# Strassen's seven products for the second layer of an attention and gelu-MLP kernel

## The chip, the core and the metric

The kernel runs on one core of one Trainium2 chip. The metric is the device time of one execution in microseconds. TensorE (PE) multiplies, VectorE (DVE), ScalarE (ACT) and GpSimd (POOL) work on tiles, and DMA queues move data, those of SyncE (SP) and of GpSimd here. Each engine takes its instructions in the order in which they were written, and waits for the others by semaphores. Operands lie in SBUF, results of TensorE in PSUM.

## The reference

Attention over 8 batches, 12 heads, 448 tokens and a head width of 64, with q and k normalised by their root mean square, and behind it a two-layer perceptron on the 3584 tokens. All inputs are float32 and the output is float32.

```python
q_n, k_n = rmsnorm(q, g_q), rmsnorm(k, g_k)
scores = 1/sqrt(64) * q_n @ k_n.T
attn = softmax(scores)                   # over keys
x = (attn @ v) as (8*448, 768)           # heads side by side
h = x @ w_in                             # 768 -> 2048
g = gelu_tanh(h)
out = g @ w_out                          # 2048 -> 768
```

## The kernel before

Tokens of a batch are taken as 7 blocks of R = 64 (token number modulo 7 gives the block), heads as three chunks of four (c = 0 to 2). Matmuls are in bfloat16. The weights `win` and `wout` stay in SBUF; `g` holds the gelus of two batches. Nearly all matmuls of the steady part use a quarter of the array, 64 rows by 64 columns, so that four of them run side by side.

The work on a batch b goes in two alternating stretches. In the **first layer** of batch b (`mm1_turn`, L537) TensorE makes eight pairs of 128 rows of h, ScalarE turns each into `g` (L543), GpSimd normalises q and k of the next batch (`normed`, L278), DMAs transpose them into `qT` and `kT`, and VectorE multiplies `kT` by the gains (`gain`, L325) and sums squares (`total`, L173). In the **attention phase** of batch b + 1 (`attention`) TensorE weaves two things together: scores and products of batch b + 1, and the second layer of batch b.

The order on TensorE in that phase is written by hand, as words of a string (`STEADY` for batches 2 to 7, `SECOND` for batch 1). `u` is one of 21 units (`unit`, L335): the scores of 64 keys of a chunk, four matmuls of 448 columns into a PSUM pair; ScalarE takes their exps (`exp`, L343). `s` and `x` (`products`, L387) are the sums of the exps and the product with V of a chunk, the latter 28 matmuls. `5r` is five steps of the second layer, four matmuls each of 384 columns (`quartered`, L495); the last 32 steps of a phase have 192 columns.

A second string gives VectorE's order for the three chunks: A, B, F and G add exps of 7 key blocks into `es` (L355, L358, L360, L362) so that `s` needs four matmuls; T transposes the sums (`turned`, L397), R takes reciprocals (L402), S spreads them (L409), M multiplies the product with V into `xT` (L422). E is an eviction of a finished second-layer tile (`evict`, L513), on VectorE or at a place in ScalarE's order given by the dict behind the strings. `go_on` writes an instruction of VectorE or ScalarE as soon as what it needs has been written (`needs`). So the words fix each engine's order, and semaphores the times.

PSUM is four pairs of banks, `rounds`. `u`, `s` and `x` take the pair at the front and put it at the back; the second layer takes one out for as long as it sums into it. Whoever takes a pair waits for its last reader: an exp, T, M or an eviction.

`follows` makes TensorE drain before the two halves of the array's rows swap their banks. `final` does the last second layer, on the whole array (L463). `gpsimd_waits` (L800) is a one-element copy that holds GpSimd back until the last add of exps in a phase.

## Time and profile before

| | before |
|---|---|
| median of 3 runs | 390.82 us (389.91 to 391.95) |
| span of the profiled execution | 389.1 us |
| TensorE busy | 381.8 us |
| ScalarE busy | 278.2 us |
| VectorE busy | 242.0 us |
| GpSimd busy | 126.1 us |
| mean granted TensorE clock | 1.000 |

The profile is of one execution, whose own device time is not listed apart from its span, from the first to the last instruction; the listed runs lie 0.8 to 2.9 us above that span. A row of a timeline gives the start, the length, the engine, the line, the operation, what it writes and reads with the shape of one, and how many instructions are merged. Matmul rows overlap, since a matmul's recorded end lies after the next one's start; what a group takes of TensorE is read from one start to the next.

### The profile page before, as it was taken

Reading aid. Unit: us, or ns where it says so; the run is one execution under the profiler, and the core shown is the slowest. Engines: PE = TensorE matmul, PEld = TensorE weight load, DVE = VectorE, ACT = ScalarE, POOL = GpSimd, SP = SyncE. Lnnn points to the kernel's source line nnn. Section 1 sums busy time; section 2 is a strip of 40 time slices with the busy share of each in tenths; the row PEclk is TensorE's granted clock in tenths of the full one; section 3 lists DMA queues with packets and bytes.
Section 4 is the critical chain, followed back from the end, with each engine's and each line's share of the span. In section 5 each row is a group of like instructions: output and inputs, shape, how many; then the busy total and the mean of one; then the engine's idle time right before and its main releaser. Section 6 shows DMA issues by size and latency. Waiting matters only on the chain.

```text
span 389.1 us, 17513 instructions
## 1 busy us (share of the span) xinstructions
PE 381.8 (98%) x8044; PEld 296.3 (76%) x8044; DVE 242.0 (62%) x367; ACT 278.2 (71%) x351; POOL 126.1 (32%) x109
## 2 busy tenths in 40 slices
...
GB/s 258 326 232 210 210 222 239 260 175 192 209 44 106 256 197 60 76 154 257 133 64 65 189 253 103 47 115 241 110 68 61 121 48 42 44 65 4 2 81 83
...
## 3 DMA queue, kind: packets, MB, share of 16 engines
...
q0 software_dynamic: 10128, 11.80, 18.3%
...
## 4 chain that ended last, share of the span: by engine, by line
PE 92%; ACT 4%; DMA 1%; POOL 1%; SPq 0%; DVE 0%; issue 0%; DVEq 0%
PE t L537 33%; PE t L495 32%; PE t L387 9%; PE t L335 7%; PE t L463 5%; PE t L556 4%; ACT ex L343 4%; DMA rawq<-in_q_dram 1%; POOL g L164 1%; PE h L436 1%; PE o L387 0%; PE tp L296 0%; SPq L750 0%; DVE ss L173 0%; PE os L387 0%
## 5 line engine op out<-in xcount | busy, mean ns | idle before, releaser
L343 ACT ACTIVATE ex<-t,shift 128x896 bf16<-128x896 f32 x168 | 156.2, 1012 | 2.6 <-PE t L335 2.1
L495 PE MATMUL t<-wout,g 64*64 64x384 bf16 (+1 forms) x3456 | 152.0, 305 | 0.0
L495 PEld LDWEIGHTS <-g 64*64 64x64 bf16 x3456 | 115.3, 107 | 17.7 <-issue 0.2
L537 PE MATMUL t<-xT,win 64*64 64x448 bf16 x2688 | 128.7, 349 | 0.0
L537 PEld LDWEIGHTS <-win 64*64 64x64 bf16 x2688 | 97.8, 107 | 29.4
L543 ACT ACTIVATE g<-t 128x896 bf16<-128x896 f32 x56 | 50.5, 915 | 56.8 <-PE t L537 56.7
L173 DVE TENSOR_REDUCE ss<-sq 128x14 f32<-128x896 f32 (+3 forms) x45 | 44.3, 999 | 48.7 <-ACT sq L162 46.4
L335 PE MATMUL t<-qT,kT 64*64 64x448 bf16 x672 | 59.7, 352 | 1.9 <-ACT ex L343 0.6
L800 POOL COPY mark<-es 1x1 bf16<-1x1 bf16 x7 | 1.2, 177 | 134.9 <-DVE es L362 126.6
L278 POOL TENSOR_TENSOR nrmq<-rawq,rinv 128x896 bf16<-128x896 f32 (+1 forms) x21 | 34.8, 1659 | 18.8 <-ACT rinv L205 8.4
L355 DVE TENSOR_TENSOR es<-ex 128x1792 bf16<-128x1792 bf16 x21 | 22.2, 1059 | 29.5 <-ACT ex L343 29.5
L278 POOL TENSOR_TENSOR nrmk<-rawk,rinv 128x896 bf16<-128x896 f32 (+1 forms) x21 | 34.6, 1647 | 0.0
L387 PE MATMUL t<-ex,vb 64*64 64x448 bf16 x588 | 32.4, 350 | 0.2 <-issue 0.2
L335 PEld LDWEIGHTS <-kT 64*64 64x64 bf16 x672 | 26.1, 106 | 8.1 <-DVE kT L305 2.0
L397 DVE STREAM_TRANSPOSE st<-t 128x448 f32<-128x448 f32 x42 | 24.8, 628 | 9.2 <-PE t L387 9.2
L387 PEld LDWEIGHTS <-vb 64*64 64x64 bf16 x672 | 23.2, 107 | 8.3 <-issue 1.8
L409 DVE STREAM_TRANSPOSE rb<-rc 128x896 f32<-128x896 f32 (+1 forms) x25 | 26.7, 1068 | 0.3
L706 DVE COPY osb<-t 128x384 f32<-128x384 f32 (+1 forms) x4 | 2.0, 508 | 35.2 <-PE t L463 35.2
L422 DVE TENSOR_TENSOR xT<-t,rb 128x896 bf16<-128x896 f32 x21 | 22.8, 1087 | 0.9
L513 ACT COPY osb<-t 128x768 f32<-128x768 f32 (+1 forms) x18 | 12.6, 700 | 14.0 <-PE t L495 14.0
L358 DVE TENSOR_TENSOR es<-es,ex 128x1792 bf16<-128x1792 bf16 x21 | 22.3, 1062 | 0.0
L164 POOL TENSOR_TENSOR sq<-rawq 128x896 f32<-128x896 f32 (+1 forms) x9 | 13.6, 1510 | 24.1 <-DVE ss L173 17.4
...
## 6 DMA issues: line engine op xcount, KB each, us to landing
...
win<-in_moe_w_in_dram POOLq DMA_DIRECT2D x8, 384.0 KB, 11.1
...
```

The costliest lines, as they stand in the source:

```text
L173: nc.vector.reduce_sum(sss[b][:, seat(b, c), "qk".index(n), hs, ts], squares(b, c, n, hs, ts), axis=AX.X)
L278: eng.tensor_mul(nrms[n, b, c][:, ts].rearrange("p t a d -> p a t d"), raws[n, b, c][:, :, ts], root[:, :, ts].to_broadcast([P, 2, m, D]),)
L335: nc.tensor.matmul(sc[r * R:(r + 1) * R, a, :S], kT[rs, c, t, r], qT[b][rs, c, :, r], start=True, stop=True,)
L343: nc.scalar.activation(exs[b, c][:, t], scs.pop((b, c, t))[:, :, :S], AF.Exp, scale=scale, bias=shift)
L358: nc.vector.tensor_add(es, es, ex[:, 4:6])
L387: nc.tensor.matmul(o[r][a * D:(a + 1) * D], vb[b % 2][rs, 2 * c + a, i] if what else ones[rs], es[i][rs, a], start=(i == 0), stop=(i == n ...
L397: nc.vector.transpose(st[:, r].rearrange("p a b -> p (a b)"), o[r])
L409: nc.vector.transpose(oas["rb"][:, rs].rearrange("p r s -> p (r s)"), rc.to_broadcast([128, (rs.stop - rs.start) * m, 32]),)
L422: nc.vector.tensor_mul(xT[b][:, 2 * c:2 * c + 2], oas["o", c, 1][:, :, :S], oas["rb"])
L495: mm = nc.tensor.matmul(o[a * R:(a + 1) * R, bank, :hi - lo], g[rs, f, at:at + R], wout[rs, f, lo:hi], start=(n == 0), stop=(n == len(step ...
L537: mm = nc.tensor.matmul(h[a * R:(a + 1) * R, j, :S], win[rs, c, at:at + R], xT[b][rs, c], start=begin and c == cs[0], stop=end and c == cs ...
L543: nc.scalar.activation(g[:, 2 * i:2 * i + 2, (b % 2) * S:(b % 2 + 1) * S], h[:, :, :S], AF.Gelu_apprx_tanh,)
```

## The change

The second layer of a batch, 448 tokens by 2048 by 768, is computed for batches 1 to 7 by Strassen's method in the form with seven products: six token blocks are halved into three and three (A1, A2), the 2048 into even and odd groups of 128, the 768 columns into halves. Seven products of half size in each direction stand for eight. The seventh token block (64 tokens) is done apart, in as many matmuls as before, with the sum of its two halves ("L") and B12 - B22. Batch 0 is done directly (`direct`), now with its last block within the same phase.

Sums of the gelus (`summands`): "S", three instructions on VectorE, "4" and "L" on GpSimd, each for halves of j: the first in the first layer, the others at the phase's head. Sums of the weights (`weight_sums`): three on GpSimd of 3072 elements a partition during the attention phase of batch 1, one on VectorE, in place, in the first layer of batch 1.

The products are combined when they are evicted: `scalar_part` (a), `vector_part` (e) and `gpsimd_part` (g), with numbers k = 0 to 3 for the products of token blocks 0 and 1 over 384 columns, 4 to 7 for the third block, 8 for the seventh block (`evict_rest`). Of the products, k = 0 holds numbers 2 and 1, k = 1 numbers 5 and 6, k = 2 numbers 3 and 7, k = 3 number 4 in two halves; 4 to 7 likewise. The steps of k = 0 to 2 are 16 each, of 384 columns; the others are eight matmuls of 192 columns a step: 8 for each of k = 3 to 6, and 20 for k = 7 and 8 together, which hold two PSUM pairs.

To make room, `g`, `xT`, `es` and V (`vb`) have one buffer each; the scratch of the first squares lies in the new tiles; V of the next batch is loaded in the first layer, on GpSimd's queue behind its multiplies.

```diff
@@ -50,13 +50,14 @@
...
-    xp = ctx.enter_context(tc.tile_pool(name="xp", bufs=2))
+    esp = ctx.enter_context(tc.tile_pool(name="esp", bufs=1))
+    xp = ctx.enter_context(tc.tile_pool(name="xp", bufs=1))
...
-    op = ctx.enter_context(tc.tile_pool(name="op", bufs=3))
+    op = ctx.enter_context(tc.tile_pool(name="op", bufs=1))
@@ -106,13 +107,23 @@
...
-    vb = [wts.tile([P, HP, NT, D], BF16, name=f"vb{i}") for i in range(2)]
+    vb = wts.tile([P, HP, NT, D], BF16, name="vb")
...
-    g = gp.tile([128, nf, 2 * S], BF16, tag="g", name="g")
+    g = gp.tile([128, nf, S], BF16, tag="g", name="g")
...
+    NJ = nf // 2
+    QD = HD // 2
+    TH = 3 * R
...
+    wt = wts.tile([128, 3, NJ, HD], BF16, name="wt")
+    sm = gp.tile([128, 3, NJ, TH], BF16, tag="sm", name="sm")
+    sp = gp.tile([128, NJ, R], BF16, tag="sp", name="sp")
@@ -472,53 +467,281 @@
...
+    def rounds_of(lanes, outs, operands, per):
...
+        left = {}
+        for lane in lanes:
+            for acc, _ in lane:
+                left[acc] = left.get(acc, 0) + 1
+        for n in range(n_all):
+            if n and any(lane[n][0] != lane[n - 1][0] for lane in lanes):
                 follows(mm)
...
-                bank = (r + turn) % 2
...
+                acc, step = lanes[r][n]
...
+    def turns(x, y, n):
+        xs, ys = [(x, i) for i in range(n)], [(y, i) for i in range(n)]
+        return [xs + ys, ys + xs]
+    def take():
+        return rounds.pop(0)
+    def give(o):
+        rounds.append(o)
+    def summands(js, eng, what):
+        a1, a2 = slice(0, TH), slice(TH, 2 * TH)
+        if "S" in what:
+            eng.tensor_sub(sm[:, 1, js], g4[:, js, 0, a2], g4[:, js, 0, a1])
+            eng.tensor_add(sm[:, 0, js], sm[:, 1, js], g4[:, js, 1, a2])
+            eng.tensor_add(g4[:, js, 0, a2], g4[:, js, 0, a2], g4[:, js, 1, a2])
+        if "4" in what:
+            eng.tensor_sub(sm[:, 2, js], g4[:, js, 1, a1], sm[:, 0, js])
+        if "L" in what:
+            eng.tensor_add(sp[:, js], g4[:, js, 0, 2 * TH:], g4[:, js, 1, 2 * TH:])
+    def weight_sums(i):
+        b11, b12 = w4[:, :, 0, :HD], w4[:, :, 0, HD:]
+        b21, b22 = w4[:, :, 1, :HD], w4[:, :, 1, HD:]
+        if i == 3:
+            nc.gpsimd.tensor_sub(wt[:, 1], b12, b22)
+        elif i == 2:
+            nc.gpsimd.tensor_sub(wt[:, 0], b11, wt[:, 1])
+        elif i == 4:
+            nc.gpsimd.tensor_sub(wt[:, 2], b21, wt[:, 0])
+        else:
+            nc.vector.tensor_sub(b12, b12, b11)
...
+    PAIRS = ((2, 1), (5, 6), (3, 7))
+    def strassen(finished):
+        k = 0
+        for wide in (True, False):
+            w = HD if wide else QD
...
+                o = take()
+                outs = {x: o[:, 0, :w], y: o[:, 1, :w]}
+                for n in rounds_of(turns(x, y, NJ), outs, operands, 1 if wide else 2):
+                    if n == (2 * NJ if wide else NJ) - 1:
+                        give(o)
+                        finished(k, o)
+                    yield
+                k += 1
+            if wide:
+                o = take()
+                outs = {(4, h): o[:, h, :QD] for h in range(2)}
+                for n in rounds_of(turns((4, 0), (4, 1), NJ), outs, operands, 2):
+                    if n == NJ - 1:
+                        give(o)
+                        finished(k, o)
+                    yield
+                k += 1
+        o4, ol = take(), take()
+        outs = {4: o4[:, 0, :QD], "l0": ol[:, 0, :QD], "l1": ol[:, 1, :QD]}
+        def operands(acc, step, rs, a):
+            if acc == 4:
+                return left_of(4, step, rs, 2), right_of(4, step, rs, a * QD, (a + 1) * QD)
+            lo = int(acc[1]) * QD
+            return rest_of(step, rs, lo, lo + QD, a)
+        quarter = [(4, j) for j in range(NJ)]
+        l0, l1 = ([(acc, n) for n in range(nf)] for acc in ("l0", "l1"))
+        lanes = [quarter + l1[:NJ] + l0 + l1[NJ:], l0[:NJ] + quarter + l1 + l0[NJ:]]
+        for n in rounds_of(lanes, outs, operands, 2):
+            if n == NJ - 1:
+                give(o4)
+                finished(k, o4)
+            if n == len(lanes[0]) // 2 - 1:
+                give(ol)
+                finished(k + 1, ol)
             yield
-    def evict(b, parts, o, eng):
...
+    def scalar_part(b, k, o):
...
+        key = "gq"[k // 4]
+        w, t = (HD, QD)[k // 4], ob(key)
+        if k % 4 == 0:
+            nc.scalar.copy(t[:, 0::3], o[:, :, :w])
+        else:
+            nc.scalar.copy(t[:, 2], o[:, 0, :w])
+    def vector_part(b, k, o):
+        key = "gq"[k // 4]
+        w, t = (HD, QD)[k // 4], ob(key)
+        if k % 4 == 1:
+            nc.vector.tensor_add(t[:, 3], o[:, 1, :w], t[:, 3])
+        elif k % 4 == 2:
+            nc.vector.tensor_add(t[:, 1::2], o[:, :, :w], t[:, 1::2])
+            rows_out(b, key, 0, [(0, 2)])
+        else:
+            if key == "g":
+                d = t[:, 3].rearrange("p (h d) -> p h d", h=2)
+                nc.vector.tensor_add(d, o[:, :, :QD], d)
+            else:
...
+    def gpsimd_part(b, k):
+        key = "gq"[k // 4]
+        t = ob(key)
+        if k % 4 == 0:
+            nc.gpsimd.tensor_add(t[:, 0], t[:, 0], t[:, 3])
+        elif k % 4 == 1:
+            nc.gpsimd.tensor_add(t[:, 1], t[:, 2], t[:, 3])
+        else:
+            nc.gpsimd.tensor_add(t[:, 2], t[:, 2], t[:, 3])
+            rows_out(b, key, 1, [(2, 1)])
@@ -569,53 +792,45 @@
...
     STEADY = (
-        "5r u 11r uu 8r uu 8r 1r u 6r u 4r u 5r uu 6r su 5r u 3r u 2r 7r uxu 4r u 5r uu 1r s 7r u"
-        " 3r uu 5r 16r x 11r s 5r x",
-        "A0 E0 B0 F0 G0 T0 R0 A1 S0 B1 F1 M0 G1 T1 R1 A2 S1 B2 F2 G2 M1 T2 R2 S2 M2",
-        {13: 1, 20: 2, 21: 3},
+        "8r u 4r u 4r u 5r u 5r u 5r u 5r u 5r u 5r u 3r s 2r u 5r u 2r x 1r u 4r u 4r u 4r u"
+        " 3r s 1r u 4r u 2r u x 1r u 4r u 4r u 10r s x",
+        "e1 A0 B0 F0 G0 e2 T0 R0 S0 e3 M0 A1 B1 F1 e5 G1 T1 R1 S1 e6 M1 A2 B2 F2 e7 G2 T2 R2"
+        " S2 M2",
+        {2: [0], 4: [1], 12: [4], 14: [5], 21: [8]},
     )
     SECOND = (
         "u 8r uu 9r u 7r uu 10r u 3r u 5r u 2r u 4r us 6r u 3r u 1r u 6r xu 4r u 5r u 1r u"
-        " 3r s 1r u 2r u 10r u 2r x 1r s 3r x",
+        " 3r s 1r u 2r u 10r u 2r x 8r s 12r x",
         "A0 L0 E0 B0 F0 G0 J0 T0 R0 a0 S0 K0 A1 M0 B1 a1 T1 A2 R1 B2 F2 S1 M1 T2 R2 S2 M2",
-        {14: 1, 21: 2},
+        {14: [1], 21: [2, 3]},
     )
@@ -640,9 +861,14 @@
...
         def go_on():
-            for queue, eng in ((vector, nc.vector), (scalar, nc.scalar), (vector, nc.vector)):
-                while queue and made.issuperset(needs(*queue[0])):
-                    run(*queue.pop(0), eng)
+            queues = ((vector, nc.vector), (scalar, nc.scalar), (gpsimd, nc.gpsimd))
+            on = True
+            while on:
+                on = False
+                for queue, eng in queues:
+                    while queue and made.issuperset(needs(*queue[0])):
+                        run(*queue.pop(0), eng)
+                        on = True
         n = {"u": 0, "s": 0, "x": 0}
...
     def final(b):
...
+        summands(slice(NJ // 2, NJ), nc.vector, "S")
+        summands(slice(NJ // 2, NJ), nc.gpsimd, "4")
+        summands(slice(0, NJ), nc.gpsimd, "L")
+        def finished(k, o):
+            if k == 8:
+                evict_rest(b, o, (nc.scalar, nc.vector))
+                return
+            if k % 4 < 2:
+                scalar_part(b, k, o)
+            if k % 4:
+                vector_part(b, k, o)
+            if k % 4 < 3:
+                gpsimd_part(b, k)
+        for _ in strassen(finished):
+            pass
@@ -882,7 +1108,7 @@
...
-            lambda: w_out_part(14, 16), lambda: load_v(1, 0, 2), lambda: load_v(1, 2, 4)),
+            lambda: w_out_part(14, 16)),
@@ -934,7 +1160,7 @@
...
-            m1 = [(0, lambda: total(1, 0, "k"),
+            m1 = [(0, lambda: load_v(1, 0, 2), lambda: load_v(1, 2, 4), lambda: total(1, 0, "k"),
@@ -954,15 +1180,18 @@
...
+            extra.append(("first", lambda: weight_sums(3)))
             extra.append(("J0", lambda: gpsimd_waits(ess[1, 0][:1, 0, 0, :1])))
             for at, n in enumerate("qk"):
                 extra += [
                     ("J0", lambda n=n: square(2, 0, n, nc.gpsimd)),
                     (f"a{at}", lambda n=n: total(2, 0, n))]
+            extra += [("J0", lambda i=i: weight_sums(i)) for i in (2, 4)]
...
+                m1.append((0, lambda: weight_sums(1)))
@@ -972,11 +1201,19 @@
...
+            m1.append((1, lambda: load_v(b + 1, 0, HP)))
             m1.append((9, lambda: gain(b + 1, 0)))
...
+        if b:
+            m1 += [(7, lambda: summands(slice(0, NJ // 2), nc.vector, "S")),
+                   (8, lambda: summands(slice(0, NJ // 2), nc.gpsimd, "4"))]
+        if b and b + 1 < B:
+            extra += [("first", lambda: summands(slice(NJ // 2, NJ), nc.vector, "S")),
+                      ("first", lambda: summands(slice(NJ // 2, NJ), nc.gpsimd, "4")),
+                      ("first", lambda: summands(slice(0, NJ), nc.gpsimd, "L"))]
         if 0 < b and b + 2 < B:
             m1.append((4, lambda: loads(b + 2, 1)))
@@ -1024,7 +1261,6 @@
...
             ends.append(lambda: rsqrt(b + 2, slice(0, NCH if b else 1)))
-            side += [(0 if b else 11, lambda: load_v(b + 2, 0, HP))]
```

240 lines of the change are left out of this document (147 added, 93 removed).

## The prediction

> **What bounds the kernel now.** I read the page first: busy times, then the chain of work that ended last, by line.
>
> ```profile
> PE 381.8 (98%) x8044; PEld 296.3 (76%) x8044; DVE 242.0 (62%) x367; ACT 278.2 (71%) x351; POOL 126.1 (32%) x109
> ```
>
> ```profile
> PE t L537 33%; PE t L495 32%; PE t L387 9%; PE t L335 7%; PE t L463 5%; PE t L556 4%; ACT ex L343 4%; DMA rawq<-in_q_dram 1%; POOL g L164 1%; PE h L436 1%; PE o L387 0%; PE tp L296 0%; SPq L750 0%; DVE ss L173 0%; PE os L387 0%
> ```
>
> TensorE is busy 98% of the span and is the chain; the second layer (L495 and L463) is 37% of it. So a matmul taken away is worth its time as long as TensorE, which issues in order, still never waits. Next the chain in order of time (start, length, what):
>
> ```profile
> 166.17 18.16 PE t L537 x384
> ...
> 185.33 1.79 PE t L495 x44
> ...
> 211.16 18.16 PE t L537 x384
> ...
> 364.47 20.96 PE t L463 x144
> ```
>
> One batch repeats every 211.16 - 166.17 = 45.0 us: 18.16 us of first layer, then 26.8 us in which scores, products and the second layer of the batch before are woven together (the attention phase). A 64x64x384 matmul costs 1.79/44 = 0.0407 us, four (one step "r") 0.163. The last batches end with 20.96 us of second layer alone. The phase's end on TensorE (window 180 to 214) prices the rest:
>
> ```profile
> 208.13 1.10 PE L495 MATMUL t<-wout,g 64*64 64x192 bf16 x44
> 209.04 0.39 PE L387 MATMUL t<-es,ones 64*64 64x448 bf16 x4
> 209.23 0.61 PE L495 MATMUL t<-wout,g 64*64 64x192 bf16 x20
> 209.64 1.52 PE L387 MATMUL t<-ex,vb 64*64 64x448 bf16 x28
> 210.97 3.38 PE L537 MATMUL t<-xT,win 64*64 64x448 bf16 x65
> ```
>
> Starts count, since ends overlap: 44 matmuls of 192 columns take 0.91 us (0.0207 each, half of a 384-column one), s 0.19, x 1.33; a unit u is four matmuls like s, 0.19.
>
> ScalarE in the same phase, which begins at about 184.15 (210.97 less a phase of 26.8):
>
> ```profile
> 184.37 0.92 ACT L543 ACTIVATE g<-t 128x896 bf16<-128x896 f32 x1 [0.22 <-PE t L537]
> 185.31 1.28 ACT L1024 ACT_TABLE_LOAD   x1
> 186.60 11.87 ACT L343 ACTIVATE ex<-t,shift 128x896 bf16<-128x896 f32 x13
> 198.34 0.82 ACT L513 COPY osb<-t 128x768 f32<-128x768 f32 x1
> 199.02 1.05 ACT L343 ACTIVATE ex<-t,shift 128x896 bf16<-128x896 f32 x1
> ```
>
> The first exp starts 2.45 us into the phase; exps follow at (198.34 - 186.60)/13 = 0.903 us, each done after 1.01; an eviction of 768 elements takes a slot of 0.68, one of 384 half of that by estimate. 21 exps are 19.0 us, so ScalarE has little to spare in 26.8. VectorE:
>
> ```profile
> 190.34 1.09 DVE L355 TENSOR_TENSOR es<-ex 128x1792 bf16<-128x1792 bf16 x1 [3.56 <-ACT ex L343]
> 191.35 0.95 DVE L513 COPY osb<-t 128x768 f32<-128x768 f32 x1
> 192.21 1.08 DVE L358 TENSOR_TENSOR es<-es,ex 128x1792 bf16<-128x1792 bf16 x1
> 193.33 0.62 DVE L360 TENSOR_TENSOR es<-es 128x896 bf16<-128x896 bf16 x1
> 194.06 0.62 DVE L362 TENSOR_TENSOR es<-es,ex 128x896 bf16<-128x896 bf16 x1
> 195.30 1.18 DVE L397 STREAM_TRANSPOSE st<-t 128x448 f32<-128x448 f32 x2 [0.62 <-PE t L387]
> 196.52 0.33 DVE L402 RECIPROCAL rc<-st 128x28 f32<-128x28 f32 x1
> 196.76 1.04 DVE L355 TENSOR_TENSOR es<-ex 128x1792 bf16<-128x1792 bf16 x1
> 197.72 1.10 DVE L409 STREAM_TRANSPOSE rb<-rc 128x896 f32<-128x896 f32 x1
> ```
>
> These are A0 E0 B0 F0 G0 T0 R0 A1 S0 (T0 is two transposes), nearly back to back: VectorE's order is a chain of its own, with TensorE running just ahead of it.
>
> **The change, part by part.**
>
> *Matmuls removed.* Before, a batch's second layer in a phase was 384 matmuls of 384 columns and 128 of 192: 15.6 + 2.65 = 18.3 us. Strassen has 192 and 416: 7.8 + 8.6 = 16.4. That is 1.85 us less in each of six phases (batches 1 to 6), 11.1 us. The first phase gains batch 0's remainder, 128 of 192 columns, +2.65. The end falls from 20.96 to 16.4 and some 0.3 for ten drains between lanes: -4.3, its evictions being spread over the products before. With TensorE never waiting: -12.7 us.
>
> *Does TensorE then wait?* In four places the written order leaves less time than the operations between need. (1) s1 follows u13 by 4r, u and 3r: 7 x 0.163 + 0.19 = 1.33 us, but exp 13 (0.3 to start, as in the u-to-exp handover estimated from T0 below, plus 1.01) and G1 (0.62) take 1.95: 0.6 short. (2) At the 80th r the product pair 6 goes back to the four PSUM buffers, two are taken for the last part, u17 gets the third and x1 that very one, which e6 must read first. In VectorE's order e6 comes after T1 R1 S1: from s1, 0.5 to reach T1, 1.22 to R1, 0.36 to S1, 1.05 and 0.54 for e6, 3.65 us, against 7 r, 3 u and s, 1.9: 1.75 short. (3) With two buffers left u19 needs M1, which reads x1: 1.33 + 0.3 + 1.09 = 2.7 against 2.35: 0.35. (4) s2 follows u20 by 10 half-column r, 1.65, against 1.95: 0.3. Together 3.0 us that no spare time elsewhere removes, already more than 1.85.
>
> The whole chain is longer, since every wait feeds the next. Counted from the phase's start: exp 5 ends at 2.45 + 5 x 0.903 + 0.68 + 0.37 (the evictions a0 and a1 now stand ahead of exp 4) + 1.01 = 9.0. B0 to F0 1.12, F0 to G0 0.73, G0 0.62: s0 at 11.5, where TensorE with 49 r and 9 u would have been at 9.7. e2 (768 elements, 0.86 as E0 above) stands ahead of T0: 12.35. T0, R0, S0, e3: 3.2, so 15.5, and u11, whose buffer e3 frees, only then. Exp 11 starts at 16.0; exp 11, a4, exp 12: 2.3; B1 at 18.3; F1 at +1.12; F1, e5 and G1 1.44: s1 at 20.9. To T1 0.5, and T1 to e6 3.15: x1 at 24.5. 1.63 to M1, 1.09: u19 at 27.2. Exp 19 ends at 28.7; B2 to G2 2.56: s2 at 31.3; s2 and x2 1.52: first layer at 32.8. Before: 26.8. So +6.0 us in each phase, 36 in six.
>
> The delays of 0.3 and 0.5 between engines are estimates: T0 starts 0.5 after s0 would (s0 just behind G0's end, 194.68), of which 0.19 is s0's own. VectorE alone, without any wait from A0 on, would still need three times A to M (about 6.7 a chunk by the rows' spacings, M as at 77.94 below) and 2.3 for the e steps, estimated from E0 by size: 22.4 us after A0 at 6.9 (exp 3's end), so M2 at 29.3. The late part of the first layer, 64 matmuls of 18.16/384 us behind its start, wants M2 at 24.9 + 3.0 = 27.9, and had it at 29.8 before; so even then a gain of a few tenths a phase.
>
> *In the first layer* TensorE's work is the same. The sums "S" (three adds of 768 elements, 0.54 each by the 896-element row) fall into VectorE's waits; "4" and "L" on GpSimd are done before their products' turn. Single g, xT, V and es cost nothing: each is rewritten after its last reader in TensorE's own order; V's load moves behind six GpSimd multiplies and lands a phase before use.
>
> *GpSimd and VectorE at once.* Until now GpSimd lay idle while VectorE added exps. What happens when they meet is seen in the gain (L325):
>
> ```profile
> 87.62 1.69 POOL L278 TENSOR_TENSOR nrmk<-rawk,rinv 128x896 bf16<-128x896 f32 x1
> ```
>
> ```profile
> 88.32 1.24 DVE L325 TENSOR_SCALAR kT<-kT,gcols 128x896 bf16<-128x896 bf16 x1
> ```
>
> It was issued at 88.32 and ended 0.25 us after the GpSimd multiply's end, 1.24 us in place of 0.46 (row 64.51 below): it waited for the whole GpSimd instruction. The new weight sums are GpSimd instructions of 3072 elements; by the 896-element row below (1.67) 5.7 us each. Two stand behind the squares in the first attention phase, where VectorE runs:
>
> ```profile
> 31.95 2.21 POOL L790 DMA_DIRECT2D wout<-in_moe_w_out_dram  x3
> ```
>
> ```profile
> 62.28 1.67 POOL L164 TENSOR_TENSOR sq<-rawk 128x896 f32<-128x896 f32 x1
> ```
>
> ```profile
> wout<-in_moe_w_out_dram POOLq DMA_DIRECT2D x2, 384.0 KB, 20.0
> ```
>
> ```profile
> 55.64 1.09 DVE L355 TENSOR_TENSOR es<-ex 128x1792 bf16<-128x1792 bf16 x1 [4.35 <-ACT ex L343]
> ...
> 64.51 0.46 DVE L325 TENSOR_SCALAR kT<-kT,gcols 128x896 bf16<-128x896 bf16 x1
> 64.90 1.07 DVE L355 TENSOR_TENSOR es<-ex 128x1792 bf16<-128x1792 bf16 x1
> ...
> 77.94 1.09 DVE L422 TENSOR_TENSOR xT<-t,rb 128x896 bf16<-128x896 f32 x1
> ```
>
> The first sum needs all of w_out, which lands at about 33.4 + 20.0 = 53.4, and holds GpSimd to 59.1; A0 (55.64) waits 3.5. The squares end 3.5 later, at 67.4; the second sum runs to 73.1 and holds the gain, the third to 78.8 and holds A1 (64.90): +13.9. From A1 to M2's end was 14.1 us and stays so, which covers the added 2.65 of matmuls: the first phase +13.5. No row shows an exp add (two operands from SBUF) meeting GpSimd. If only the gain is held, A1 is 5 late: +5. I take +13.5, since the gain is the nearest row, and keep 5.
>
> [...]
>
> *Sum.* The span is 389.1 and the runs' median 390.8, 1.7 above it; I carry that. 390.8 + 36.0 + 13.5 - 4.3 = 436.0 us.
>
> **The rivals.**
> - *TensorE never waits* (faster): 390.8 - 12.7 = 378.1. For it: 98% on TensorE, and 192-column steps at exactly half price. Against: the four places above. It decides while the waits of a phase stay under 12.7/6 = 2.1 us, and needs VectorE to free PSUM far ahead of e6 and M1. 0.05.
> - *Only the four certain waits*, no chain: 45.0 - 1.85 + 3.0, +1.15 a phase, 6.9; +5, -4.3: 398. It needs s0 and u11 not to wait, so exps faster than 0.903. 0.07.
> - *VectorE's own pace, no waits between engines*: some 0.3 less a phase, +5 and -4.3: 389.7, no change. 0.02.
> - *GpSimd doesn't hold the exp adds*: 390.8 + 36.0 + 5 - 4.3 = 427.5. 0.22.
> - *Half the chain*: buffers come free sooner than I count (other order on VectorE, shorter handovers), 3.0 a phase with the lock as forecast: 418. 0.13.
> - *Worse*: "4", "L" or the g adds held by VectorE's adds and so late themselves; 1.5 us more a phase gives 445; 0.06.
>
> The forecast has 0.45.
>
> **How the numbers follow.** Likeliest 436. The range leaves out the first three rivals (0.14): from half the chain with only the gain held (390.8 + 18 + 5 - 4.3 = 409.5) to the worse rival and 4 us for the first phase's bounds (449). A measurement can tell about 0.5% (2 us) from no change. Faster than that 0.05, within it 0.02, slower 0.93.
>
> **What would show it.** Right: TensorE's share falls to some 85%; waits on TensorE before s (on G, L362), x1 (on the e adds of VectorE) and units (on VectorE and ScalarE); the 384-matmul first-layer pieces 51 us apart; at 60 to 80 us a gain and exp adds of several us on VectorE while GpSimd's weight sums run; from the last first layer's end to the kernel's end 20.4 us. Wrong: pieces 43 us apart with TensorE near 98% (the first rival), 46 (the second), exp adds of 1.07 beside running weight sums (the third).

## The result: 468.26 us, and the profile after

| | before | after |
|---|---|---|
| median of the runs | 390.82 us (389.91 to 391.95) | 468.26 us (466.97 to 470.86) |
| ratio to before, 95% interval | | 1.198 (1.194 to 1.202) |
| span of the profiled execution | 389.1 us | 469.1 us |
| mean granted TensorE clock | 1.000 | 0.956 |

The kernel is 20% slower. The forecast was 436.0 us with a range up to 449.0: the sign was right, the size was not. Of the runs below, one of the four of `four_on_vector` (469.71 us) lay more than 1.5% above its fastest; its ratio leaves that run out, its median of 462.38 does not (461.64 without it). The page of the changed kernel (busy times, granted clock in 40 slices, chain by engine), and the chain of the kernel before:

```profile
PE 407.4 (87%) x9212; PEld 286.8 (61%) x9212; DVE 314.3 (67%) x443; ACT 288.1 (61%) x364; POOL 214.6 (46%) x175
PEclk9999986899898999999999999899978999989999
PE 48%; ACT 15%; DVE 13%; issue 9%; POOL 6%; DMA 6%; SPq 2%; DVEq 0%; POOLq 0%; ACTq 0%
```

```profile
PE 92%; ACT 4%; DMA 1%; POOL 1%; SPq 0%; DVE 0%; issue 0%; DVEq 0%
```

TensorE is busy 87% (forecast some 85%); its share of the chain fell from 92% to 48%, and ScalarE, VectorE, issue, GpSimd and DMA have most of the rest. The largest waits of TensorE (total us, times, longest):

```profile
PE t L346 <- ACT ex L354: 17.6, 18, 3.7
PE t L398 <- DVE es L373: 15.6, 17, 1.7
```

Units wait for the exp that reads their PSUM pair, and s for VectorE's adds. By the starts of the first-layer pieces the time divides as follows (each start is the first row of L760 of a batch, or of the same line in the other kernels; before: 75.8 and then every 45.0 or 45.2):

| | start, batch 1 | 1 to 2 | 2 to 3 | 3 to 4 | 4 to 5 | 5 to 6 | 6 to 7 | last start to end |
|---|---|---|---|---|---|---|---|---|
| before | 75.8 | 45.2 | 45.0 | 45.0 | 45.0 | 45.2 | 45.0 | 43.0 |
| after | 95.2 | 57.9 | 54.3 | 52.7 | 54.2 | 58.0 | 53.4 | 43.4 |
| more than before | 19.4 | 12.8 | 9.3 | 7.7 | 9.2 | 12.8 | 8.4 | 0.4 |
| forecast of that | 13.5 | 6.0 | 6.0 | 6.0 | 6.0 | 6.0 | 6.0 | -4.3 |

The differences add up to the 80.0 us by which the span grew; the forecast's to 45.2. The 34.8 us between them are the first phase (5.9), the step to batch 2 (6.8), the five later steps (17.4) and the end (4.7).

**First phase.** The timeline between 53 and 82 us, and the window 72 to 82 (columns: busy time and instructions of PE, PEld, DVE, ACT, POOL; granted clock; DMA share; GB/s):

```profile
53.75 6.00 POOL L524 TENSOR_TENSOR wt<-wout 128x3072 bf16<-128x3072 bf16 x1 [8.81 <-DMA wout<-in_moe_w_out_dram]
55.62 5.08 DVE L366 TENSOR_TENSOR es<-ex 128x1792 bf16<-128x1792 bf16 x1 [4.35 <-ACT ex L354]
67.58 5.98 POOL L526 TENSOR_TENSOR wt<-wout,wt 128x3072 bf16<-128x3072 bf16 x1
68.38 5.43 DVE L336 TENSOR_SCALAR kT<-kT,gcols 128x896 bf16<-128x896 bf16 x1
73.64 6.02 POOL L528 TENSOR_TENSOR wt<-wout,wt 128x3072 bf16<-128x3072 bf16 x1
73.74 6.87 DVE L366 TENSOR_TENSOR es<-ex 128x1792 bf16<-128x1792 bf16 x1
```

```profile
72.00:82.00 10.00, 4.18 (x49) 2.23 (x53) 10.00 (x4) 2.01 (x2) 7.58 (x2) 0.54 0.17 60
```

A0, the gain and A1 were issued while a weight sum of 6 us ran on GpSimd, and each ended 0.25 to 0.95 us behind that sum's end: 5.08, 5.43 and 6.87 us in place of 1.09, 0.46 and 1.07. So an exp add is held like a gain. A1 ends at 80.61 instead of 65.97, 14.6 us late (forecast 13.9). TensorE is busy 4.18 of the window's 10 us, and its clock is 0.54 there.

**A steady phase**, that from 225.55 us (18.18 after the start of the first layer at 207.37):

```profile
231.88 1.15 POOL L720 TENSOR_TENSOR og<-og 128x384 f32<-128x384 f32 x1
...
233.06 0.56 DVE L702 TENSOR_TENSOR og<-t,og 128x384 f32<-128x384 f32 x1 [0.89 <-POOL og L720]
...
233.66 0.48 ACT L695 COPY og<-t 128x384 f32<-128x384 f32 x1 [1.25 <-DVE og L702]
234.03 2.81 ACT L354 ACTIVATE ex<-t,shift 128x896 bf16<-128x896 f32 x3
...
238.51 0.38 PE L398 MATMUL t<-es,ones 64*64 64x448 bf16 x4 [0.28 <-DVE es L373]
...
248.20 0.38 PE L398 MATMUL t<-es,ones 64*64 64x448 bf16 x4 [1.71 <-DVE es L373]
...
251.81 1.52 PE L398 MATMUL t<-ex,vb 64*64 64x448 bf16 x28
...
258.60 0.38 PE L398 MATMUL t<-es,ones 64*64 64x448 bf16 x4 [0.67 <-DVE es L373]
...
260.11 1.14 PE L760 MATMUL t<-xT,win 64*64 64x448 bf16 x20
```

From the phase's start s0 comes at 12.96 us (forecast 11.5), s1 at 22.65 (20.9), x1 at 26.26 (24.5), s2 at 33.05 (31.3), the next first layer at 34.56 (32.8). From s0 on the forecast's chain stands within 0.3 us; 1.5 us are lost ahead of s0. There g0 on GpSimd ends at 233.03, e1 waits for it, a1 for e1 (1.25 us), and exp 4 starts 8.5 us into the phase instead of 7.1.

The same three distances in all six phases, named by the columns above:

| us | 1 to 2 | 2 to 3 | 3 to 4 | 4 to 5 | 5 to 6 | 6 to 7 | forecast |
|---|---|---|---|---|---|---|---|
| phase's start to s0 | 17.25 | 14.48 | 12.96 | 13.44 | 17.01 | 12.77 | 11.5 |
| s0 to s1 | 9.64 | 9.68 | 9.69 | 9.69 | 9.95 | 9.69 | 9.4 |
| s1 to s2 | 11.34 | 10.41 | 10.40 | 11.34 | 11.34 | 11.26 | 10.4 |

So most of what the forecast missed in these phases lies ahead of s0.

**The end.** The first row of the last second layer, and the copy of its last block:

```profile
443.83 0.97 PE L489 MATMUL t<-wout,g 64*64 64x384 bf16 x17
...
464.08 0.32 ACT L663 COPY ol<-t 128x192 f32<-128x192 f32 x1 [6.26 <-PE t L489]
```

TensorE takes 20.2 us (forecast 16.7) until the seventh block's copy can begin at 464.08, and 5.0 us follow to 469.1 (before 3.7).

### The profile page after: what moved, and what is told of

The parts are those of the page before. It is cut to its first block, busy times and chain, and to the rows that moved or that the text cites. A ratio compares the mean times of both kernels' runs of the same rounds, so it can differ in the third digit from the quotient of the medians.

```text
span 469.1 us, 20158 instructions
## 1 busy us (share of the span) xinstructions
PE 407.4 (87%) x9212; PEld 286.8 (61%) x9212; DVE 314.3 (67%) x443; ACT 288.1 (61%) x364; POOL 214.6 (46%) x175
## 4 chain that ended last, share of the span: by engine, by line
PE 48%; ACT 15%; DVE 13%; issue 9%; POOL 6%; DMA 6%; SPq 2%; DVEq 0%; POOLq 0%; ACTq 0%
PE t L760 17%; PE t L489 15%; ACT ex L354 12%; PE t L398 7%; PE t L346 4%; DMA rawk<-in_k_dram 4%; PE t L779 3%; DVE es L369 3%; DVE es L373 2%; POOL nrmk L289 1%; DVE es L366 1%; POOL sp L517 1%; DMA kT<-nrmk 1%; DMA rawq<-in_q_dram 1%; DVE sm L512 1%
## 5 line engine op out<-in xcount | busy, mean ns | idle before, releaser
L354 ACT ACTIVATE ex<-t,shift 128x896 bf16<-128x896 f32 x168 | 163.1, 1009 | 49.6 <-PE t L346 48.5
L489 PE MATMUL t<-wout,g 64*64 64x192 bf16 (+1 forms) x2304 | 135.1, 291 | 6.0 <-DVE g L513 3.2
L760 PE MATMUL t<-xT,win 64*64 64x448 bf16 x2688 | 128.5, 349 | 0.0
L489 PEld LDWEIGHTS <-g 64*64 64x64 bf16 x3200 | 101.1, 109 | 37.1 <-PE t L489 12.0
L760 PEld LDWEIGHTS <-win 64*64 64x64 bf16 x2688 | 93.9, 107 | 33.2
L766 ACT ACTIVATE g<-t 128x896 bf16<-128x896 f32 x56 | 50.4, 914 | 62.3 <-PE t L760 62.2
L489 PE MATMUL t<-wt,sm 64*64 64x192 bf16 (+1 forms) x896 | 81.4, 304 | 2.3 <-issue 0.3
L489 PEld LDWEIGHTS <-sm 64*64 64x64 bf16 x1344 | 49.6, 116 | 21.7 <-PE t L489 11.2
L515 POOL TENSOR_TENSOR sm<-g,sm 128x768 bf16<-128x768 bf16 x14 | 25.2, 1798 | 49.6 <-DVE sm L512 49.5
L489 PE MATMUL t<-wt,g 64*64 64x192 bf16 x896 | 45.3, 247 | 0.5
L489 PE MATMUL t<-wout,sm 64*64 64x384 bf16 (+1 forms) x448 | 44.9, 317 | 0.0
L289 POOL TENSOR_TENSOR nrmq<-rawq,rinv 128x896 bf16<-128x896 f32 (+1 forms) x21 | 35.1, 1672 | 11.3 <-DVE rinv L273 5.4
L511 DVE TENSOR_TENSOR sm<-g 128x768 bf16<-128x768 bf16 x14 | 12.2, 870 | 34.7 <-ACT g L766 34.7
L366 DVE TENSOR_TENSOR es<-ex 128x1792 bf16<-128x1792 bf16 x21 | 32.5, 1546 | 4.3 <-ACT ex L354 4.3
```

Source lines behind the costliest of these rows:

```text
L289: eng.tensor_mul(nrms[n, b, c][:, ts].rearrange("p t a d -> p a t d"), raws[n, b, c][:, :, ts], root[:, :, ts].to_broadcast([P, 2, m, D]),)
L354: nc.scalar.activation(exs[b, c][:, t], scs.pop((b, c, t))[:, :, :S], AF.Exp, scale=scale, bias=shift)
L366: nc.vector.tensor_add(es, ex[:, :2], ex[:, 2:4])
L489: mm = nc.tensor.matmul(outs[acc][a * R:(a + 1) * R], lhs, rhs, start=acc not in seen, stop=not left[acc],)
L515: eng.tensor_sub(sm[:, 2, js], g4[:, js, 1, a1], sm[:, 0, js])
L760: mm = nc.tensor.matmul(h[a * R:(a + 1) * R, j, :S], win[rs, c, at:at + R], xT[b][rs, c], start=begin and c == cs[0], stop=end and c == cs ...
```

## The experiments

Times are medians, with the ratio to the kernel before and its interval; "1 to 2" and so on are the columns of the table above.

**The weight sums.** Two ways to end the long hold, `sums_on_vector` and `sums_in_pieces`.

```diff
-            nc.gpsimd.tensor_sub(wt[:, 0], b11, wt[:, 1])      # and so the two others
+            nc.vector.tensor_sub(wt[:, 0], b11, wt[:, 1])
-            extra += [("J0", lambda i=i: weight_sums(i)) for i in (2, 4)]
+            extra += [(at, lambda i=i: weight_sums(i)) for at, i in (("K0", 2), ("a1", 4))]
```

> The three weight sums of the first attention phase go from GpSimd to VectorE (sum 3 at the head, sum 2 with K0, sum 4 with a1). Theory (GpSimd's long sums hold VectorE's adds and gains): a sum of 3072 elements takes VectorE about 1.8 us (1792 elements took 1.08), sum 3 ends before A0 is due, sums 2 and 4 cost the chain at most 3.6; A0 and A1 take 1.1 us again, TensorE's long pause at 72 to 82 us goes and with it the half clock there; the first layer of batch 1 starts near 79 us instead of 95.3, the kernel takes 452 us. Rival (the phase is long through the order of words and the batch 0 remainder, not through the hold): it stays near 95 us and 468.

Measured: 455.69 us, 1.166 (1.160 to 1.172); first layer of batch 1 at 80.5.

```diff
+    def pieces(dst, x, y):
+        for j in range(NJ):
+            nc.gpsimd.tensor_sub(dst[:, j], x[:, j], y[:, j])
-            nc.gpsimd.tensor_sub(wt[:, 0], b11, wt[:, 1])      # and so the two others
+            pieces(wt[:, 0], b11, wt[:, 1])
```

> Each of the three weight sums stays on GpSimd but is written as eight instructions of 384 elements. Theory A (VectorE is held for the one running GpSimd instruction, and gets in between two): a piece is about 0.8 us, each of A0, the gain, A1, B1, F1, G1 loses up to 0.8; no VectorE add above 1.9 us; first layer of batch 1 near 84 us, 457 us in all. Theory B (GpSimd keeps what it holds from one instruction to the next while it has work): no change, 95 us and 468. If the hold has nothing to do with it: 468 as well, with adds of 5 to 7 us still there.

Measured: 453.71 us, 1.164 (1.158 to 1.170); batch 1 at 79.7. The timelines of the two:

```profile
64.73 1.75 DVE L526 TENSOR_TENSOR wt<-wout,wt 128x3072 bf16<-128x3072 bf16 x1
66.40 1.08 DVE L366 TENSOR_TENSOR es<-ex 128x1792 bf16<-128x1792 bf16 x1
```

```profile
52.70 0.91 POOL L521 TENSOR_TENSOR wt<-wout 128x384 bf16<-128x384 bf16 x1 [0.88 <-DMA wout<-in_moe_w_out_dram]
...
63.76 17.90 POOL L521 TENSOR_TENSOR wt<-wout,wt 128x384 bf16<-128x384 bf16 x16
...
64.83 1.80 DVE L366 TENSOR_TENSOR es<-ex 128x1792 bf16<-128x1792 bf16 x1
```

Without the long holds 14.7 and 15.5 us of the 19.4 go, as the theory of the hold has it. With pieces VectorE gets in between two of them (the A1 that took 6.87 takes 1.80), though GpSimd runs one behind the other; theory B is out. A1 starts at 64.83 there, as before (64.90), so the 3.9 us that stay lie behind it.

**The head of the steady phases.** `four_on_vector` gives "4" and "L" at the phases' head to VectorE; `combo` is that, the sums in pieces, and ScalarE's part written first:

```diff
-                      ("first", lambda: summands(slice(NJ // 2, NJ), nc.gpsimd, "4")),
-                      ("first", lambda: summands(slice(0, NJ), nc.gpsimd, "L"))]
+                      ("first", lambda: summands(slice(NJ // 2, NJ), nc.vector, "4")),
+                      ("first", lambda: summands(slice(0, NJ), nc.vector, "L"))]
```

```diff
-            queues = ((vector, nc.vector), (scalar, nc.scalar), (gpsimd, nc.gpsimd))
+            queues = ((scalar, nc.scalar), (vector, nc.vector), (gpsimd, nc.gpsimd))
```

> The sums 4 (second half of j) and L at the head of the phases of batches 2 to 7 go from GpSimd to VectorE. Theory (g0 stands behind squares, 4 and L on GpSimd; e1 waits for g0, a1 for e1, and the exps for a1): g0 follows a0 at once, some 3 us sooner, the 1.7 us wait of ScalarE before a1 goes; VectorE gets 0.95 us at its head; the period falls by about 1.2 us from 53.4, six phases 7 us: 461. Rival (the phase is set by the chain exp, exp adds, s, spread, e that the forecast counted, which does not start with g0): no change or 1 us more a phase, 468 to 474.

> Three edits at once: weight sums in eight pieces each, sums 4 and L of the phases' heads on VectorE, and ScalarE's part of a finished product written ahead of VectorE's (so a1 and a5 no longer wait for e1 and e5). Theory (what stands ahead of exp 4, namely g0 on GpSimd, e1 and then a1, is what made every steady phase 1.5 to 1.8 us longer than the forecast already at s0): s0 comes 11.6 us after the phase's start instead of 13.0, a1 waits for nobody but TensorE, the steady period falls from 53.5 to about 52.2, the first layer of batch 1 starts at 79.7; about 443 us. Rival (exps and VectorE's adds alone set s0): s0 at 12.5 or later, 53.4 stays, 449.

Measured: `four_on_vector` 462.38 us, 1.183 (1.178 to 1.187), with 57.0, 52.6, 53.5, 53.6, 52.6 and 53.5; `combo` 448.52, 1.147 (1.144 to 1.151), with 59.1, 52.5, 53.5, 53.0, 52.4 and 53.0. In `four_on_vector` a1 waits 1.06 to 1.17 us for e1 in the five steady phases instead of 1.07 to 3.33, and s0 comes at 12.8 to 12.9 us in all of them instead of 12.8 to 17.0:

```profile
177.26 0.48 ACT L695 COPY og<-t 128x384 f32<-128x384 f32 x1 [1.06 <-DVE og L702]
```

That is the theory's reason, though a raw load was late in that execution too (GpSimd waited 3.33 us for raw q before 221.06). But a1 still waits for e1: the steps other than 58.0 fell by 0.5 us on average (53.65 to 53.2) and not by 1.2, and most of the rest is 58.0, which became 52.6. That `combo` gave so little is seen in its timeline, in the phase from 368.17 and in that from 209.19:

```profile
375.82 4.77 ACT L354 ACTIVATE ex<-t,shift 128x896 bf16<-128x896 f32 x5
...
376.65 1.77 POOL L726 TENSOR_TENSOR og<-og 128x384 f32<-128x384 f32 x1 [2.35 <-DVE og L706]
...
377.77 1.60 DVE L369 TENSOR_TENSOR es<-es,ex 128x1792 bf16<-128x1792 bf16 x1 [0.20 <-ACT ex L354]
...
380.81 0.38 PE L398 MATMUL t<-es,ones 64*64 64x448 bf16 x4 [0.79 <-DVE es L373]
```

```profile
211.39 1.99 POOL L175 TENSOR_TENSOR sq<-rawk 128x896 f32<-128x896 f32 x1
...
211.88 1.92 DVE L512 TENSOR_TENSOR sm<-sm,g 128x768 bf16<-128x768 bf16 x1
```

Exp 4 starts at 7.65 us instead of 8.5, a1 no longer waits for e1 (it waits 0.41 us for TensorE); but now g1 on GpSimd runs beside B0, which takes 1.60 us instead of 1.09, and s0 comes at 12.64. In the other phase the squares (L175) hold the second sum of S for 1.92 us. A hold was removed and the next one took its place. `squares_moved` is `combo` and takes these squares to ScalarE, behind M0; in the phase of batch 2 it also writes the gain of chunk 1 behind S:

```diff
             for n in "qk":
+                if b:
+                    extra += [("M0", lambda n=n: square(b + 2, 2, n, nc.scalar)),
+                              ("M0", lambda n=n: total(b + 2, 2, n))]
+                    continue
                 m1.append((13, lambda n=n: square(b + 2, 2, n, nc.gpsimd)))
...
```

> On top of combo, in all phases of batches 2 to 6: the squares of the third chunk go from GpSimd at the head of the phase to ScalarE behind M0, their sums on VectorE with them. Theory (in combo the sums S still take 1.5 to 1.9 us each in place of 0.55, because the squares hold them, so that TensorE waits at product pair 1 and the gain of combo was only 0.5 a phase): S takes 0.55 each, s0 comes 11.5 us after the phase's start, the period falls from 52.9 to 51.5; 440 us. Rival (what is gained at the head is lost in the middle, where ScalarE gets 1.9 us and VectorE 2.1 us more): 53, 446.

Measured: 455.41 us, 1.164 (1.161 to 1.166), steady steps 53.0 to 54.6: the rival. s0 comes at 12.64 in all five steady phases, but in four of them s1 follows 10.7 us later instead of 9.7. It is 6.9 us slower than `combo`, more than the 5.2 that `combo` had gained over `sums_in_pieces`.

**The combining adds**, of one column each:

```diff
-            nc.vector.tensor_add(t[:, 3], o[:, 1, :w], t[:, 3])        # likewise the other e and g adds
+            nc.vector.tensor_add(t[:, 3, :1], o[:, 1, :1], t[:, 3, :1])
```

> The adds that combine the products at eviction, e on VectorE and g on GpSimd, are kept in their places but take one column each, so most of the output is not computed. Theory (they stand in the chain of the phase: e2, e3, e5, e6 with 0.9, 0.5, 0.3 and 0.5 us, and g0 ahead of e1 and a1 with 1.1): 2.3 us less in each steady phase, 51.0; six phases 14 us, 454. Rival 1 (the phase is set by exps and TensorE's words alone): within 1 us of 53.4, 466. Rival 2 (they are the whole loss): 46, 424.

Measured: 456.71 us, 1.169 (1.167 to 1.172); steady steps 51.7 to 52.8, s0 at 12.4. So without these adds a steady phase is 1.7 us shorter on average (forecast 2.3), and not 8. Part of the 1.7 is that no late s0 and fewer half-rate stretches fell into this execution: against a steady phase without either, s0 comes 0.4 us earlier, s1 follows 0.2 and s2 0.3 us sooner.

**The order of the words.** `order_only` writes `STEADY` anew; `order_combo` has the same strings on top of `combo`.

```diff
-        "8r u 4r u 4r u 5r u 5r u 5r u 5r u 5r u 5r u 3r s 2r u 5r u 2r x 1r u 4r u 4r u 4r u"
-        " 3r s 1r u 4r u 2r u x 1r u 4r u 4r u 10r s x",
-        "e1 A0 B0 F0 G0 e2 T0 R0 S0 e3 M0 A1 B1 F1 e5 G1 T1 R1 S1 e6 M1 A2 B2 F2 e7 G2 T2 R2"
-        " S2 M2",
-        {2: [0], 4: [1], 12: [4], 14: [5], 21: [8]},
+        "4r u 7r u 5r u 17r u 1r u 2r u 1r u 6r uu 8r u 1r s 2r u 5r u 3r u 2r ux 7r u"
+        " 5r u 2r su 2r uu 4r u 7r u 2r x 7r sx",
+        "e1 A0 B0 F0 G0 e2 T0 e3 R0 A1 S0 B1 M0 F1 G1 e5 T1 e6 R1 S1 A2 B2 F2 e7"
+        " G2 M1 T2 R2 S2 M2",
+        {3: [0, 1], 14: [4, 5], 21: [8]},
```

> Only the three strings of STEADY are written anew: the units earlier and in clusters, e3 before R0, A1 before S0, e6 before R1, M1 behind G2, s1 and x1 later on TensorE; every instruction is the same. Theory (of the 8 us that a steady phase is longer, a part is only the order in which engines wait for each other): with a1 still behind e1, the period falls from 53.4 to 51.3, the kernel to 456. Rival (the operations themselves fill the phase): 53 to 54, 468.

> The same new order together with the three edits of the run combo (weight sums in pieces, 4 and L on VectorE, ScalarE's part written first). Theory: with a0 and a1 early and waiting for nobody, and e6 and s1 where their inputs are ready, the steady period falls from 52.9 to 47.5 us, less than the forecast's 51.0 that was worked out for the written order; the kernel takes about 420 us. Rival (GpSimd's squares of the third chunk at the head of the phase hold the sums S whatever the order): 50 to 51, 434.

Measured: `order_only` 451.74 us, 1.154 (1.149 to 1.159), steps 54.2, 51.2, 52.3, 51.1, 50.4 and 50.4; `order_combo` 421.69, 1.079 (1.076 to 1.081), steps 54.6, 48.2, 49.4, 48.2, 48.1 and 48.1. The phase of `order_combo` from 297.94 us (18.18 behind its first layer's start at 279.76):

```profile
310.46 0.38 PE L398 MATMUL t<-es,ones 64*64 64x448 bf16 x4 [0.35 <-ACT ex L354]
...
318.56 0.38 PE L398 MATMUL t<-es,ones 64*64 64x448 bf16 x4
...
326.36 0.36 PE L398 MATMUL t<-es,ones 64*64 64x448 bf16 x4
```

s0 is at 12.52 us, hardly earlier than in `combo` (12.64), but s1 follows 8.10 us later instead of 9.69, and s2 7.80 instead of 10.4. Of the 8.6 us that a steady step is longer (53.65 on average without 58.0, against 45.0) 2.6 went with the order alone and 5.2 with order and head together, 0.8 with the head alone. With every operation still there, these were waits that the order made. The 3.4 us that are left over the kernel before were not tested.

**Drains.** Ten drains of TensorE stand in the last second layer; here 38 more.

```diff
-            if n and any(lane[n][0] != lane[n - 1][0] for lane in lanes):
+            if n and (any(lane[n][0] != lane[n - 1][0] for lane in lanes) or last and n % 4 == 2):
                 follows(mm)
```

> In the last second layer, 38 drains of TensorE are added to the ten that it has, in the middle of lanes; nothing else changes. The forecast gave a drain 0.03 us. If that was its error at the end (25.1 us measured from the last first layer to the kernel's end, 20.4 forecast), a drain costs about 0.25 us as the gaps between lanes show, and this section takes 25.1 + 9.5 = 34.6, the kernel 478. If drains are cheap and the gaps come from the evictions behind them: 25.1 + 1.1, 469.

Measured (two runs): 479.81 us, 1.228 (1.223 to 1.233); from the last first layer to the end 34.1 us instead of 25.1. 9.0/38 = 0.24 us for a drain. A gap between lanes of the changed kernel says the same, 0.32 us where rows otherwise follow by 0.08:

```profile
460.00 0.24 PE L489 MATMUL t<-wout,sp 64*64 64x192 bf16 x1
...
460.32 0.27 PE L489 MATMUL t<-wt,g 64*64 64x192 bf16 x3
```

A steady phase has ten drains too. In the phase from 225.55 us, nine of them lengthen the way from one step to the next by 0.23 us, as here (0.40 us from the first row to the second, where 0.16 is usual), and the one directly behind a unit by 0.08:

```profile
230.50 0.74 PE L489 MATMUL t<-wt,sm 64*64 64x384 bf16 x4
230.90 0.35 PE L489 MATMUL t<-wout,g 64*64 64x384 bf16 x2
```

That is 2.2 us, more than the 1.85 that Strassen's fewer matmuls save in a phase. The kernel before had four switches of the halves in a phase, and its strings put two units (or an x) at each. At the first one, the eight matmuls of two units take their usual 0.38 us and the second layer goes on without a gap:

```profile
186.92 0.58 PE L335 MATMUL t<-qT,kT 64*64 64x448 bf16 x8
187.30 1.50 PE L495 MATMUL t<-wout,g 64*64 64x384 bf16 x32
```

An order that covers the ten new switches in this way was not tried.

**The clock.** In the changed kernel, s1 waits 1.71 us for G1 in the phase from 278.3 us; three windows of 3.41 us about that wait, and one that has part of the same wait ahead of 248.20:

```profile
301.42 0.59 PE L398 MATMUL t<-es,ones 64*64 64x448 bf16 x4 [1.71 <-DVE es L373]
```

```profile
297.98:301.39 3.41, 1.66 (x62) 1.21 (x53) 2.52 (x4) 2.22 (x4) 0.68 (x2) 1.00 0.09 20
301.39:304.80 3.41, 3.31 (x64) 2.41 (x67) 2.62 (x4) 1.79 (x3) 0.47 (x1) 0.51 0.02 5
304.80:308.21 3.41, 2.75 (x76) 2.00 (x66) 1.23 (x2) 2.25 (x3) 0.59 (x1) 0.99 0.25 57
246.85:250.26 3.41, 1.81 (x55) 1.26 (x58) 2.86 (x7) 2.13 (x3) 0.59 (x1) 1.00 0.00 0
```

In the second window the clock is at a half (0.51), in the three others whole (1.00, 0.99 and 1.00); behind the last it stays whole (1.00 from 250.26 to 253.67). By windows of 0.1 us this trace has eight half-rate stretches up to the last matmul, six of 3.41 us, one of 6.83 and one of 13.65. The wait for s1 is 1.71 us in all six phases; in four of them a stretch of 3.41 begins up to 1.2 us behind the wait's end. TensorE was busy 1.63 us of the 3.41 ahead of 301.42, and 1.63 of the 3.41 ahead of 248.20 too: why the clock fell behind the one and not behind the other is not shown. `zeros_in_waits` fills part of the waits before u6 and s1 with matmuls by zeros.

```diff
+    zero = consts.tile([128, R], BF16)
...
+            state['pad'] = lambda r, a, n=n: nc.tensor.matmul(
+                outs[lanes[r][n][0]][a * R:(a + 1) * R], zero[r * R:(r + 1) * R],
+                operands(*lanes[r][n], slice(r * R, (r + 1) * R), a)[1], start=False, stop=False,
+            )
...
```

> In every steady phase 24 matmuls by a block of zeros, into the sum then open, stand ahead of the unit u6 (about 1 us of its wait of 1.7 to 2.1) and 48 of 192 columns ahead of s1 (1 us of its 1.7). They add nothing to the result. Theory A (TensorE's pauses halve its clock for stretches of 3.41 us, and that half speed lies on the path): the clock is 1.00 from batch 2's first layer on, and the kernel takes 3 to 8 us less, 462. Theory B (the half-clock stretches lie where TensorE waits for others anyhow): clock near 1.00, time the same within 2 us, 468. If zeros do not count as work for the clock, it stays at 0.95 in the same places.

Measured: 462.98 us, 1.186 (1.183 to 1.190); steps 56.1, 53.2, 53.6, 53.0, 53.5 and 52.6. The granted clock, which has one deep stretch left, in the first phase:

```profile
PEclk9999995899999999999999999999999999999999
```

More work, and 5.3 us less by the medians: theory A. The traces show where. In the changed kernel, s2 follows s1 by 11.3 us in the four phases in which a half-rate stretch lies behind the wait for s1 (1 to 2, 4 to 5, 5 to 6, 6 to 7), and by 10.4 in the two without one. With the zeros it is 10.1 to 10.4 in all six. So a stretch there costs 0.9 us, the four of them 3.7. The first layer of batch 1 also started 1.7 us earlier in this execution, though the edit doesn't touch what is ahead of it. At full clock a step is still 53.2 on average, so the clock isn't what makes a steady phase 8 us longer.

**The step of 58.0 us (batch 5 to 6).** Its phase began with GpSimd waiting 5.25 us for raw q. Behind these squares stand "4", "L" and g0, and a1 waits 3.33 us for e1, which waits for g0:

```profile
333.52 1.67 POOL L175 TENSOR_TENSOR sq<-rawq 128x896 f32<-128x896 f32 x1 [5.25 <-DMA rawq<-in_q_dram]
...
342.64 0.48 ACT L695 COPY og<-t 128x384 f32<-128x384 f32 x1 [3.33 <-DVE og L702]
```

So s0 comes at 17.01 us, and exp 4 in it 10.6 us behind the phase's start. `v_later` issues V's load later.

```diff
-            m1.append((1, lambda: load_v(b + 1, 0, HP)))
+            m1.append((12, lambda: load_v(b + 1, 0, HP)))
```

> The load of the next batch's V is issued behind slot 12 of the first layer instead of slot 1. Theory (in the phase of batch 6, 58.6 us instead of 53.4, the raw q and k of the third chunk land late because V's 672 KB are moved at the same time): that phase becomes 53.4, the kernel 463. Rival (the transposes that stand before these loads on SP's queue make them late): 58.6 stays, 468; if V then comes late for the product of the first chunk, more.

Measured: 465.30 us, 1.191 (1.186 to 1.195); that step 53.5. But it is 52.4 to 55.5 in the other kernels with the given `STEADY` too, which load V early, so the run doesn't show that V was the cause. Why the load was late in this execution stays open; that it delays s0 by way of g0 is what the rows and `four_on_vector` show.

**The step to batch 2.** It takes 53.4 to 61.0 us in every changed kernel. In the changed kernel's phase of batch 2, S stands behind a gain of 3.66 us, which GpSimd's two squares hold, and TensorE waits 2.26 us for S. `second_phase` (on `sums_in_pieces`) puts S ahead of a gain there and two squares on ScalarE; `order_head` does this on `order_combo` and moves the gain of chunk 2 behind M0; `order_head_v` moves V's load as well.

```diff
-            if b == 1:
-                extra.append(("first", lambda: gain(2, 1)))
-            else:
+            if b > 1:
                 m1.append((14, lambda: gain(b + 1, 1)))
...
+        if b == 1:                                             # behind S, not ahead of it
+            extra.append(("first", lambda: gain(2, 1)))
...
+                if b == 1:
+                    extra += [("M0", lambda n=n: square(b + 2, 2, n, nc.scalar)),
+                              ("M0", lambda n=n: total(b + 2, 2, n))]
+                    continue
...
-            extra.append(("first", lambda: gain(b + 1, 2)))    # this only in order_head and order_head_v
+            at = (len(extra), "first") if b > 1 else (0, "M0")
+            extra.insert(at[0], (at[1], lambda: gain(b + 1, 2)))
```

> On top of sums_in_pieces, in the phase of batch 2 alone: the sums S stand ahead of the gain of chunk 1 on VectorE, and the two squares of the third chunk of batch 3 go from GpSimd, where they ran at the head of that phase, to ScalarE behind M0. Theory (that phase takes 59.1 us, 5.6 more than the next, because S stands behind a gain that GpSimd's squares hold, and TensorE waits for S): 54 us, the kernel 449. Rival (late transposes and late raw loads make it long): 58 or more, 453.

> On top of order_combo, in the phase of batch 2 alone: S ahead of the gain of chunk 1, the third chunk's squares from GpSimd to ScalarE behind M0, and the gain of chunk 2 behind M0 too. Theory (that phase is long because VectorE, which takes its list in order, stands at gains that wait for GpSimd and for transposes, with S, e1 and through them TensorE and ScalarE behind it): 54.6 falls to about 50 us, the kernel to 417. Rival (the transposes and V land too late for the units and products themselves): 54 or more.

> order_head, with the load of V behind slot 12 of the first layer in all batches. If V's transfer is what makes the transposes of the third chunk land late in batch 2's phase: that phase another 1 to 2 us shorter, and no steady phase above 48.5 us (order_combo had one of 49.4 where the raw loads came late): 414. If V then lands too late for the first product: a wait at x0 and more than 417.

Measured: 458.13 us, 1.167 (1.160 to 1.175), step 60.4; 424.79, 1.087 (1.084 to 1.089), step 57.3; 423.61, 1.084 (1.078 to 1.091), step 56.3. The theories fell: without the edits the step was 59.1 (`sums_in_pieces`) and 54.6 (`order_combo`), so the new head made it 1.3 and 2.7 us longer, and V's later load gave back 1.0. The timeline of `order_head` shows the lateness earlier, in the first layer of batch 1:

```profile
94.22 2.00 POOL L289 TENSOR_TENSOR nrmk<-rawk,rinv 128x896 bf16<-128x896 f32 x1
...
94.71 1.93 DVE L512 TENSOR_TENSOR sm<-sm,g 128x768 bf16<-128x768 bf16 x1
...
96.56 2.04 DVE L513 TENSOR_TENSOR g<-g 128x768 bf16<-128x768 bf16 x1
98.52 1.07 DVE L184 TENSOR_REDUCE ss<-sq 128x14 f32<-128x896 f32 x1
...
99.63 1.04 ACT L173 ACTIVATE sq<-rawk 128x448 f32<-128x448 f32 x2 [2.65 <-DVE ss L184]
...
100.58 1.71 ACT L770 ACTIVATE g<-t 128x896 bf16<-128x896 f32 x2
```

S is held by GpSimd's multiplies (the first row is one), a sum of squares stands behind S, ScalarE's square waits 2.65 us for that, and the last two gelus end at 102.3, some 4.7 us after TensorE's last first-layer matmul (79.4 + 18.2). So S of the first half is written last in this layer:

```diff
-            m1 += [(7, lambda: summands(slice(0, NJ // 2), nc.vector, "S")),
-                   (8, lambda: summands(slice(0, NJ // 2), nc.gpsimd, "4"))]
+            m1 += [(7 if b > 1 else 15, lambda: summands(slice(0, NJ // 2), nc.vector, "S")),
+                   (8 if b > 1 else 15, lambda: summands(slice(0, NJ // 2), nc.gpsimd, "4"))]
```

> order_head, and in the first layer of batch 1 alone the sums S and 4 of the first half are written behind everything else of that layer. Theory (S, held by GpSimd's multiplies, pushes a sum of squares, ScalarE's square and the last gelus back): the last gelu of batch 1 ends 0.9 us after TensorE's last first-layer matmul as in the other batches instead of 3.6, no half clock follows, and the period from batch 1 to batch 2 falls from 57.3 to 51; the kernel to 417. Rival (the raw loads, which land late, hold ScalarE's squares and so the gelus anyway): 55 or more.

> order_combo, with the sums S and 4 of the first half written last in the first layer of batch 1 alone. Same theory: from 54.6 to 51 or 52, the kernel to 418; here S of both halves then stands behind the gain of chunk 1, which GpSimd's squares held for 3.87 us, so 53 if that holds TensorE.

Measured: `order_s_late` 420.45 us, 1.078 (1.075 to 1.080), step 53.4; `order_s_late_b`, without the edits of `order_head`, 424.39, 1.088 (1.085 to 1.091), step 57.0. The row of the last gelus in `order_s_late`:

```profile
98.14 1.71 ACT L770 ACTIVATE g<-t 128x896 bf16<-128x896 f32 x2
```

They end at 99.9, and the mean clock is 0.999. With the head of `order_head`, the place of S in that first layer is worth 3.9 us of the step (57.3 to 53.4). But `order_combo`, with neither edit, had 54.6: both together gain 1.2 us, and either alone loses 2.4 to 2.7. The 5 us that are left over the other steps stay open.

No version beats the kernel before; the best is 420.45 us, and `order_combo` with 421.69 doesn't differ from it beyond the intervals.

## Why the prediction was wrong, step by step

- *Matmuls removed, -1.85 us a phase, and -4.3 at the end.* The count was right, the drains were not. At the end ten were put at 0.3 us together; they cost 2.4. Those 2.1 are part of the 4.7 us missed at the end; 1.3 more lie behind TensorE, where the copies and stores of the last block come after all else; the rest are waits of some tenths between the products. In a phase the forecast gave the drains nothing; they take 2.2 us there, where the old order hid its four. In the measured phases they must mostly fall into time in which TensorE would wait anyway, since from s0 on the chain comes out right without them; but the rival without waits was not 378.1 in this written order: with these numbers, 12.7 less 6 x 2.2 less 2.1, it comes out 2.6 us above the kernel before, at some 393 by estimate.
- *The chain of a steady phase, +6.0.* The likeliest case was right in kind: in the written order, VectorE's and ScalarE's adds and evictions hold TensorE. It measured +7.7 at the least, +8.6 on average without the 58.0. The step that failed is "exp 5 ends at 9.0", from which s0 at 11.5 follows: it counted two evictions ahead of exp 4, but not that a1 comes behind e1, and e1 behind g0 on GpSimd. In the phase shown exp 5 ends at 10.4. "'4' and 'L' on GpSimd are done before their products' turn" was true; that g0 stands behind them, and behind squares that wait for raw q and k, was not seen. Some 13 of the 17.4 us missed in the five later steps lie ahead of s0. Taking the wait of a1 away (`combo`) was worth 0.8 us a step, since B0 then met g1 and s0 still came at 12.6; an s0 of 11.5 was never reached. From s0 on the waits came as written, but for the clock: x1 3.6 us behind s1 as forecast, s2 6.8 behind x1 as forecast.
- *"S falls into VectorE's waits."* Wrong in part. In the steady first layers its adds take 0.56 us as forecast. But all three in the first layer of batch 1, and one or two at the head of four phases, are held by GpSimd's multiplies and squares and take 1.3 to 2.0 us. In `order_head` the early S of batch 1 made the gelus late. What makes the step to batch 2 +12.8 instead of +6.0 in the changed kernel lies mostly ahead of s0 too (17.25 us); S and the gain that is held ahead of it are seen there, but no run shows what each is worth.
- *The first phase, +13.5.* The hold and its places were right (A0, gain, A1), and the choice between +13.5 and +5 too: without it 15.5 us go. "The lock" in the rival "half the chain" is this hold: no run shows a lock, the runs show two adds and a gain of 5.08 to 6.87 us that end 0.25 to 0.95 us behind GpSimd's sum. The sums took 6.0 us each, not 5.7. Wrong was that "A1 to M2's 14.1 us covers the added 2.65": 3.9 us stay when the hold is gone and A1 is on time.
- *The clock.* No term. Some 41 us ran at half rate, (1 - 0.956) x 2 x 469.1, of which 17 lie about the hold of the first phase. The four stretches behind s1's waits cost 3.7 us; what the others cost is not shown.
- *The range* ended at 449.0, because "worse" was given 1.5 us a phase. Three causes with one sign, the drains at the end, the holds ahead of s0 and the clock, were each left at next to nothing.
